# Paired output products in a segment-recurrent transformer kernel, and a new order of its first tiles

## The chip, the cores and the metric

The kernel runs on one core of a Trainium2 chip. The metric is the device time of one launch in microseconds (us), less being better. Each kernel is run several times, and the median is told; in addition one execution is recorded by the hardware profiler. The engines of the core are TensorE (PE; its weight loads are listed as PEld), VectorE (DVE), ScalarE (ACT), GpSimd (POOL) and SyncE (SP). SP, ACT and POOL also issue DMA transfers. SBUF is the on-chip memory of 128 partitions; PSUM holds the results of products[...].

## The reference: what is computed

The input `x` has 2048 rows of 1024 columns in bf16. It is normalized once (`xn`), and two branches work on `xn`: a recurrent attention, and an MLP with 3584 hidden columns. The output is the sum of `x` and both branches.

```python
# attention: 64 segments of 32 rows, 8 memory rows carried from one to the next
for s in range(n_seg):
    h = concat([mem, xs])                                   # 8 + 32 rows
    q, k, v = h @ Wq, h @ Wk, h @ Wv                        # 32 heads of 128
    p = softmax(where(mask, q @ k.T * scale, -1e9))
    o = (p @ v) @ Wo                                        # sum over 32 heads
    mem = o[:8];  outs.append(o[8:])
# MLP
h = gelu(xn @ w1 + b1);  b = h @ w2 + b2
return x + attention(xn) + b
```

Segment s + 1 needs the first eight rows of segment s's output. So the 64 segments run one after the other, and each reads all of `Wq`, `Wk`, `Wv` and `Wo` (32 MB).

## The kernel before

**Two stages.** First comes the MLP, in four groups of 512 rows (`for tg in range(4)`, L488). Each group has 28 blocks `fb` of 128 hidden columns (L507 to L529: eight products into one PSUM bank, then ScalarE and VectorE compute the gelu) and then the product with `w2`. Its result, with `x` and `b2` added, goes to memory and comes back later as `res`, the residual of a segment. Then come the 64 segments (L691).

**Start.** The first four tiles of 128 rows are normalized (L462 to L478): statistics by `bn_stats` on VectorE (L351), the square root on ScalarE (L355), the reciprocal on VectorE (L361), and the scaling, for tiles 0 to 2 on ScalarE (`ln_apply_scalar`, L378) and for tile 3 on VectorE (`ln_apply`, L365). TensorE turns each tile by eight transposes (L387), and VectorE and ScalarE copy the halves out of PSUM (L390). The products of the first block (L510) read all four tiles.

**Units and streams.** The weights are cut into 64 units of 128 x 2048 (512 KB each): 16 each of K, Q, V and O. Of these, 46 stay in SBUF. Eighteen don't fit and are read again in each segment through six places (`STREAM_BUFS`); two of them lie in PSUM banks (`kept`) and are copied by VectorE into their place (`copy_bits`, L244), two copies each. `unit_done` (L675) runs when a unit's products are issued: the place is given to the next stream (`start_stream`), whose DMA is issued from SP and waits for TensorE to have read the old one. Of the sixteen O units, numbers 3, 5, 7, 10, 13 and 14 are streamed; 14 is one of the two kept ones.

**A segment.** K, Q and V each make two half passes of eight units. A unit is four products of 512 columns (`product`, L709, issued at L715), each with 32 rows of the result in another quarter of the partitions (`tile_position`), so that the four run side by side. The 32 rows of a pass are the eight memory rows and 24 of the segment's own. Its other eight rows ("left" rows) are handled for four segments at a time: for each half pass, one segment of four makes a second set of products for them. `i4` is the segment's number modulo 4. Scores, the softmax and `values` (L883) are placed between units, through the lists `at`.

**The O stage** (L1006 to L1017). Sixteen units, each for two heads (k = 0 and 1), are summed in one PSUM bank `psX`. In 17 segments (`left_o`: i4 = 1, and the last one) the stationary operand has 64 rows, and a unit is four products of 512 columns in two halves of the partitions. In the other 47 it has 32 rows, and a unit is eight products of 256 columns, four for each head:

```python
(w, i, u), n = unit, 512 if left_o else 256                              # L911
for k in range(2):
    for jq in range(DM // n):
        r, c0 = n // 8 * jq, DM * k + n * jq                             # row, column
```

Between these units stand the `values` of the second half of the heads, whose results (L905: one copy on ScalarE, one on VectorE) are the stationary operand from unit 8 on. With i4 = 3 VectorE also copies the left rows of V at unit 9 (`left_values`, L770).

**From a segment to the next.** After the last unit, ScalarE copies `psX` as bf16 into `o_sb` (L1022). TensorE first makes some products of the next segment ahead that don't need the memory rows (`lead_products`, up to six units for left rows, three of them ahead of `put_mem`), then `put_mem` (L289) turns the eight memory rows, VectorE copies them into `hT` (L293), and the next segment's K products start. VectorE adds `psX` to `res` (L1037), and GpSimd stores the rows (L1070). At the very end twelve stores are issued from SP, ACT and POOL in turn (L1059).

**Order.** The program's order is the written order on each engine (`manual_schedule`), and each engine works through its own list. Three PSUM banks `acc` are shared by all passes: `new_acc` takes the one that was given back first, `let_go` gives one back.

Of the kernel before, what the change touches and what calls it, by code (L numbers as in the profile page):

```python
# [10 lines left out]
BF16 = mybir.dt.bfloat16  # L11
U32 = mybir.dt.uint32
F32 = mybir.dt.float32
ACT = mybir.ActivationFunctionType
ALU = mybir.AluOpType
PSUM = bass.MemoryType.PSUM

P = 128
# [35 lines left out]
STREAM_BUFS = 6  # L54
AT_BANKS, AT_PART = 5, 4
# [32 lines left out]
def kernel(  # L88
# [211 lines left out]
    with tc.tile_pool(name="ma", bufs=2) as ma, tc.tile_pool(name="mps", bufs=6, space=PSUM) as mps:  # L300
# [27 lines left out]
        load_w1(range(2))  # L328
        nc.sync.dma_start(out=b1rows[:, :], in_=B_b1.rearrange("(fc p) -> fc p", p=P))
        load_w1(range(2, 6))  # L330
# [17 lines left out]
        def ln_stats(tt, xt):  # L348
            stats = ma.tile([P, 2, 6], F32, name="ln_stats")
            for c in range(2):  # L350
                nc.vector.bn_stats(out=stats[:, c, :], in_=xt[:, c * 512:c * 512 + 512])  # L351
            nc.vector.bn_aggr(out=mv[:, tt, :], in_=stats[:, :, :])
# [18 lines left out]
        def ln_apply_scalar(tt):  # L371

            xn = ma.tile([P, DM], BF16, name="ln_xn")
            shift = mv[:, tt, 0:1]
            nc.vector.tensor_scalar(
                out=shift, in0=shift, scalar1=rstd[:, tt:tt + 1], scalar2=-1.0, op0=ALU.mult, op1=ALU.mult,
            )
            nc.scalar.activation(  # L378
                out=xn[:, :], in_=xtoks[tt], func=ACT.Identity, bias=shift, scale=rstd[:, tt:tt + 1],
            )  # L380
            return xn

        def turn_x(tt, xn, xnT):
            t = tt % 4
            pT = mps.tile([P, KT, P], BF16, name="pT", bufs=2)
            for kt in range(KT):
                nc.tensor.transpose(pT[:, kt, :], xn[:, kt * P:(kt + 1) * P], ident)  # L387
            for half in range(2):
                cp = nc.scalar.copy if (tt + half) % 2 else nc.vector.tensor_copy
                cp(  # L390
                    out=xnT[half][:, 4 * t:4 * t + 4, :, :].rearrange("p s k t -> p k s t"),
                    in_=pT[:, 4 * half:4 * half + 4, :].rearrange("p k (s t) -> p k s t", t=SEG),
                )
# [68 lines left out]
        def begin(tt):  # L462
            ln_stats(tt, xtoks[tt])
            ln_sqrt(tt, tt + 1)

        def normed(tt):
            ln_rstd(tt, tt + 1)
            return ln_apply_scalar(tt) if tt < 3 else ln_apply(tt)

        begin(0)  # L470
        xns = []
        for tt in range(4):
            if tt < 3:
                begin(tt + 1)
            xns.append(normed(tt))
            if tt > 0:
                turn_x(tt - 1, xns[tt - 1], xnT)
        turn_x(3, xns[3], xnT)  # L478
# [9 lines left out]
        for tg in range(4):  # L488
# [18 lines left out]
            for fb in range(FC):  # L507
                ps = mps.tile([P, 512], F32, name="ps")
                for kt in range(KT):
                    nc.tensor.matmul(  # L510
                        ps[:, :].rearrange("p (s t) -> p s t", t=SEG),
                        lhsT=w1_sb[fb // 2][:, kt, (fb % 2) * P:(fb % 2 + 1) * P],
                        rhs=xnT[kt // 4][:, :, kt % 4, :],
                        start=(kt == 0),
                        stop=(kt == KT - 1),
                    )
# [28 lines left out]
            if not last:  # L545
# [7 lines left out]
                for t in range(4):  # L553
                    ln_stats(4 * tg + 4 + t, xtoks[4 * tg + 4 + t])
# [66 lines left out]
    with tc.tile_pool(name="late", bufs=1) as late, \  # L621
# [16 lines left out]
        def let_go(ps):  # L638
            free_banks.append(bank_of.pop(id(ps))[0])
# [51 lines left out]
        for s in range(NSEG):  # L691
# [216 lines left out]
            def o_product(unit, t, acc):  # L908


                (w, i, u), n = unit, 512 if left_o else 256  # L911
                lhs = outs[i // 4] if left_o else outs[i // 4][:, :, m0:m0 + SEG]
                for k in range(2):
                    for jq in range(DM // n):
                        r, c0 = n // 8 * jq, DM * k + n * jq
# [192 lines left out]
```

## Time and profile before

| What | us |
|---|---|
| Median of 3 runs | 1869.29 (1865.07 to 1869.99) |
| Profiled execution, its own time | 1868.06 |
| Its span, first to last instruction | 1866.3 |
| First product of the first MLP block | at 15.99 |
| First product of segment 0 | at 419.35 |
| PE busy | 1720.2 (92%) |
| PEld busy | 938.3 (50%) |
| DVE busy | 905.1 (48%) |
| ACT busy | 649.4 (35%) |
| POOL busy | 286.7 (15%) |

In the profile a row of a timeline has the start, the duration, the engine, the line, the operation, its operands as "out<-in" with their shapes, the count of instructions merged in the row, and in brackets how long the engine was idle before it and what ended that. A row of the waits tells who waited for whom: the total in us, how often, and the longest. "issue" is idle time that ended without any event that the profile shows. "DMA" in the page's slices is the busy share of the 16 DMA engines, in tenths, in 40 equal slices of the span.

### The profile page before, as it was taken

The numbers are of one execution on the slowest core, as the hardware profiler recorded it, in microseconds if no ns is written. First come the engines' busy times: TensorE is split into PE (matmuls) and PEld (weight loads), VectorE is DVE, ScalarE is ACT, GpSimd is POOL, SyncE is SP. The second block draws the span as 40 slices with busy tenths as digits, with TensorE's granted clock in tenths as the row PEclk, the third lists the DMA queues.
The fourth block names the chain that finished last, engine by engine and source line by source line (L and its number), as shares of the span: only waits on it lengthen the run. The fifth ranks groups of instructions, "written<-read, shape, count | busy, mean of one in ns | idle before, by whom it ended". The sixth has DMA issues, their size and how long they took to land.

```text
span 1866.3 us, 72877 instructions
## 1 busy us (share of the span) xinstructions
PE 1720.2 (92%) x32208; PEld 938.3 (50%) x32228; DVE 905.1 (48%) x2192; ACT 649.4 (35%) x1382; POOL 286.7 (15%) x563
## 2 busy tenths in 40 slices
PE   7999999999999999998899999999898898999987
PEld 3444444445555555555554555555555454545544
DVE  6657483705444444444444444444444444445443
ACT  6434251602333333333333333333333333333333
POOL 0000001401341121111111111111111111111112
PEclk9999999999999999999999999999999999999999
DMA  9921212769999999999999999999999999999998
GB/s 290 311 83 47 54 46 60 255 217 388 401 394 380 395 390 384 387 380 371 369 383 368 390 388 390 365 384 374 379 389 360 369 368 377 387 389 394 388 381 315
DMA packets 229353, 613.13 MB, mean 329 GB/s; under 512 B 46859, under 2 KB 76091, under 8 KB 229036
## 3 DMA queue, kind: packets, MB, share of 16 engines
q1 hardware_dynamic: 207260, 588.06, 83.8%
q0 software_dynamic: 17536, 17.71, 2.9%
q8 instruction: 252, 4.13, 0.9%
q10 hardware_dynamic: 4240, 2.71, 0.5%
q14 instruction: 65, 0.53, 0.1%
HBM read 594.40 MB, written 29.23 MB: 334 GB/s over the span
## 4 chain that ended last, share of the span: by engine, by line
PE 40%; DMA 20%; issue 4%; DVE 4%; ACT 2%; POOL 0%; DVEq 0%; ACTq 0%; SPq 0%; POOLq 0%
PE acc L715 27%; PE acc L919 9%; DMA u<-Wc_K 8%; DMA u<-Wc_O 7%; DMA outL_d<-half_home 2%; PE acc L891 1%; DMA u<-Wc_Q 1%; ACT mixed L865 1%; DVE b_oL L780 1%; PE mixed L824 1%; DVE pd_main L872 1%; DMA u<-Wc_V 1%; DMA hr_home<-hr_d 1%; ACT mixed L862 0%; PE mixed L830 0%
## 5 line engine op out<-in xcount | busy, mean ns | idle before, releaser
L715 PE MATMUL acc<-u,hr_home 128*32 128x512 bf16 x11520 | 781.3, 381 | 36.6 <-issue 13.8
L715 PEld LDWEIGHTS <-hr_home 128*32 128x32 bf16 x12288 | 353.3, 96 | 321.8 <-issue 69.7
L715 PE MATMUL acc<-u,hrL 128*32 128x512 bf16 x2880 | 258.7, 383 | 7.7 <-issue 7.3
L510 PE MATMUL ps<-u 128*128 128x512 bf16 x896 | 195.5, 381 | 2.6 <-ACT u L390 2.6
L244 DVE TENSOR_SCALAR u<-kept 128x512 uint32<-128x512 uint32 x254 | 163.4, 685 | 33.1 <-PE acc L715 11.1
L919 PE MATMUL acc<-u,d_oL 128*32 128x256 bf16 (+1 forms) x3108 | 157.6, 290 | 22.5 <-DMA u<-Wc_O 12.8
L565 PE MATMUL ps<-u 128*128 128x512 bf16 x657 | 146.2, 379 | 0.8
L919 PEld LDWEIGHTS <-b_oL 128*32 128x32 bf16 x3569 | 112.8, 98 | 67.4 <-issue 36.7
L1070 POOL DMA_DIRECT2D out_dram<-hr_home x188 | 96.3, 513 | 310.3 <-DVE hr_home L1037 296.9
L510 PEld LDWEIGHTS <-u 128*128 128x128 bf16 x896 | 88.1, 98 | 108.8 <-issue 4.8
L919 PEld LDWEIGHTS <-d_oL 128*32 128x32 bf16 (+1 forms) x3552 | 104.4, 98 | 74.9 <-issue 34.9
L872 DVE TENSOR_TENSOR pd_main<-half_home,mixed 128x320 bf16<-128x320 bf16 x128 | 62.5, 488 | 153.5 <-ACT mixed L865 152.2
L919 PE MATMUL acc<-u,b_oL 128*32 128x256 bf16 (+2 forms) x2062 | 119.9, 289 | 18.4 <-DMA u<-Wc_O 10.6
L266 POOL DMA_DIRECT2D hr_home<-hr_d x58 | 32.8, 565 | 589.3 <-PE acc L715 570.0
L780 DVE STREAM_TRANSPOSE b_oL<-b_oL 128x512 bf16<-128x512 bf16 x128 | 90.6, 708 | 63.0 <-ACT b_oL L766 63.0
L715 PEld LDWEIGHTS <-hrL 128*32 128x32 bf16 x3072 | 91.8, 96 | 58.3 <-issue 22.3
L766 ACT CAST kT<-acc 128x512 bf16<-128x512 f32 x64 | 37.5, 586 | 217.2 <-PE acc L715 217.2
L766 ACT CAST b_oL<-acc 128x512 bf16<-128x512 f32 x128 | 75.2, 587 | 83.6 <-PE acc L715 82.6
L565 PEld LDWEIGHTS <-u 128*128 128x128 bf16 x672 | 65.3, 98 | 77.4 <-DVE g_u L526 0.4
L1022 ACT CAST d_oL<-acc 128x256 bf16<-128x256 f32 (+1 forms) x63 | 26.9, 427 | 211.8 <-PE acc L919 211.8
L518 ACT ACTIVATE g_xb<-ps,b1col 128x512 bf16<-128x512 f32 x112 | 76.8, 686 | 60.4 <-PE ps L510 59.3
L865 ACT ACTIVATE mixed<-mixed,small_consts 128x160 f32<-128x160 f32 x256 | 94.2, 368 | 8.4
(127 smaller groups left out, 2004.7 us busy)
## 6 DMA issues: line engine op xcount, KB each, us to landing
u<-Wc_K SPq DMA_DIRECT2D x320, 512.0 KB
u<-Wc_V SPq DMA_DIRECT2D x256, 512.0 KB
u<-Wc_O SPq DMA_DIRECT2D x256, 512.0 KB
u<-Wc_Q SPq DMA_DIRECT2D x128, 512.0 KB
u<-Wc_O SPq DMA_DIRECT2D x64, 320.0 KB
u<-in_B_w_dram SPq DMA_DIRECT2D x28, 512.0 KB
hr_home<-hr_d POOLq DMA_DIRECT2D x58, 128.0 KB, 5.5
u<-in_A_Wq_dram SPq DMA_DIRECT2D x14, 512.0 KB
```

The costliest lines, as they stand in the source:

```text
L244: nc.vector.tensor_single_scalar(out=out, in_=in_, scalar=0, op=ALU.bitwise_or)
L266: eng.dma_start(out=hr_home[:, 0:n], in_=hr_d[s, :, 0:n])
L510: nc.tensor.matmul(ps[:, :].rearrange("p (s t) -> p s t", t=SEG), lhsT=w1_sb[fb // 2][:, kt, (fb % 2) * P:(fb % 2 + 1) * P], rhs=xnT[kt // ...
L518: nc.scalar.activation(out=xb[:, :], in_=ps[:, :], func=ACT.Identity, bias=b1col[:, fb:fb + 1], scale=1.0)
L565: nc.tensor.matmul(ps[:, :], lhsT=gts[fc // 4][:, fc % 4, t * P:(t + 1) * P], rhs=w2_sb[fc // 2][:, fc % 2, cs], start=(fc == 0), stop=(fc ...
L715: nc.tensor.matmul(o, lhsT=lhs[:, i, :], rhs=m, start=(i == seq[0]), stop=(i == seq[-1]), tile_position=(0, 32 * j),)
L766: cp(out=out, in_=ps.rearrange("p (h e) -> p h e", e=32))
L780: nc.vector.transpose(out=home, in_=home)
L865: nc.scalar.activation(out=mixed[:, 160 * b:160 * b + 160], in_=mixed[:, 0:160], func=ACT.Exp, scale=-1.0, bias=off[:, b:b + 1],)
L872: nc.vector.tensor_tensor(out=pdA.rearrange("p c b q -> p b c q"), in0=prA[:, None, :, :].to_broadcast([P, 2, 4, 40]), in1=dd, op=ALU.mult,)
L919: nc.tensor.matmul(acc[r:r + n // 8, c:c + wide], lhsT=lhs[:, 4 * (i % 4) + 2 * u + k, :], rhs=w_t[:, c0 + c:c0 + c + wide], start=(unit = ...
L1070: nc.gpsimd.dma_start(out=out_flat[rows, 256 * j:256 * j + 256], in_=res[32 * j:32 * j + NX, :])
```

## The change

- In the 47 segments that are not `left_o`, O units 0 to 8 (`NPAIR = 9`) are four products of 512 columns. Head k = 0 is summed in partitions 0 to 63 of the bank and head k = 1 in 64 to 127; each product takes 32 partitions and two 256-column blocks of the weights (`r` and `r + 2`) through a strided operand. Units 9 to 15 are eight products of 256 columns as before, into a second bank.
- Ahead of unit 9 `fold` adds the two halves of the first bank: two ScalarE copies and two VectorE additions of 64 x 256 into an f32 tile `folded` in SBUF. At the end VectorE adds the second bank and `folded` into `o_sb`, where ScalarE copied before, and `res` is added to `o_sb` and no longer to PSUM.
- All four first tiles are scaled on VectorE; the statistics are computed by half tiles, and the next tile's half stands between. Sixteen products of the identity (`WARM`) are issued first and never read. The first three MLP blocks are made in halves: the 256 columns of tiles 0 and 1 for two blocks ahead of tile 3's transposes, for the third after them, and then the other halves.
- The bias rows' load stands after the first `w1` tile and not after two. The last stores are issued from SP and ACT alone.

```diff
-        load_w1(range(2))
+        load_w1(range(1))
         nc.sync.dma_start(out=b1rows[:, :], in_=B_b1.rearrange("(fc p) -> fc p", p=P))
-        load_w1(range(2, 6))
+        load_w1(range(1, 6))
...
+        idle = new_ps()
+        for _ in range(WARM):
+            nc.tensor.matmul(
+                idle.rearrange("p (a b) -> p a b", b=P), lhsT=ident, rhs=ident[:, None, :].to_broadcast([P, 4, P]),
+                start=True, stop=True,
+            )
+        begun = [new_ps() for _ in range(3)]
+        ln_stats(0)
+        ln_half(1, 0)
+        ln_sqrt(0, 1)
+        pTs = []
         for tt in range(4):
+            ln_rstd(tt, tt + 1)
+            pTs.append(turned(ln_apply(tt)))
             if tt < 3:
-                begin(tt + 1)
-            xns.append(normed(tt))
-            if tt > 0:
-                turn_x(tt - 1, xns[tt - 1], xnT)
-        turn_x(3, xns[3], xnT)
+                ln_half(tt + 1, 1)
+                turned_out(tt, pTs[tt], 0, xnT, nc.scalar.copy)
+                ln_sqrt(tt + 1, tt + 2)
+                turned_out(tt, pTs[tt], 1, xnT, nc.scalar.copy)
+            if tt < 2:
+                ln_half(tt + 2, 0)
+            if tt == 2:
+                for fb in range(2):
+                    first_product(begun[fb], fb, xnT, 0, 8)
+        turned_out(3, pTs[3], 0, xnT, nc.vector.tensor_copy)
+        turned_out(3, pTs[3], 1, xnT, nc.scalar.copy)
+        first_product(begun[2], 2, xnT, 0, 8)
...
+                if tg == 0 and fb < len(begun):
+                    ps = begun[fb]
+                    first_product(ps, fb, xnT, 8, 16)
+                else:
+                    ps = new_ps()
+                    first_product(ps, fb, xnT, 0, 16)
...
+                for k in range(2):
+                    if left_o:
+                        tiles = [(64 * r, 64, (2 * r, 2 * r + 1)) for r in range(2)]
+                        start, stop = n == 0 and k == 0, n == 15 and k == 1
+                    elif n < NPAIR:
+                        tiles = [(64 * k + 32 * r, 32, (r, r + 2)) for r in range(2)]
+                        start, stop = n == 0, n == NPAIR - 1
+                    else:
+                        tiles = [(32 * r, 32, (r,)) for r in range(4)]
+                        start, stop = n == NPAIR and k == 0, n == 15 and k == 1
+                    for r0, rows, blocks in tiles:
+                        for c, wide, cols in o_columns(unit, t, k, blocks):
                             nc.tensor.matmul(
-                                acc[r:r + n // 8, c:c + wide],
+                                acc[r0:r0 + rows, c:c + wide],
                                 lhsT=lhs[:, 4 * (i % 4) + 2 * u + k, :],
-                                rhs=w_t[:, c0 + c:c0 + c + wide],
...
+            def fold(ps):
+                t = sp.tile([P, 256], F32, name="folded", tag="a")
+                for b in range(2):
+                    nc.scalar.copy(out=t[64 * b:64 * b + 64, :], in_=ps[64:128, 256 * b:256 * b + 256])
+                for b in range(2):
+                    q = slice(64 * b, 64 * b + 64)
+                    nc.vector.tensor_tensor(out=t[q, :], in0=ps[0:64, 256 * b:256 * b + 256], in1=t[q, :], op=ALU.add)
+                let_go(ps)
+                return t
...
+                if n == NPAIR and not left_o:
+                    st["folded"] = fold(psX)
+                    psX = new_acc()
+                o_product(n, t, psX)
...
-                nc.scalar.copy(out=o_sb[:, 0:no, :], in_=psX[:, 0:32 * no].rearrange("p (h e) -> p h e", e=32))
+                o = psX[:, 0:32 * no].rearrange("p (h e) -> p h e", e=32)
+                if left_o:
+                    nc.scalar.copy(out=o_sb[:, 0:no, :], in_=o)
+                else:
+                    folded = st["folded"].rearrange("p (h e) -> p h e", e=32)
+                    nc.vector.tensor_tensor(out=o_sb[:, 0:no, :], in0=o, in1=folded, op=ALU.add)
...
-                engines = [nc.sync, nc.scalar, nc.gpsimd]
+                engines = [nc.sync, nc.scalar]
```

## The prediction

> **What bounds the kernel now.** I read the page's slices first, then the stretches, the waits, and the timeline of one segment and of the first 20 us. The profiled execution took 1868.06 us: a span of 1866.3 and 1.76 around it. It lies 1.2 below the median of the runs shown.
>
> From the page: DMA by slice, and the instruction queue (packets, MB, share).
>
> ```profile
> DMA  9921212769999999999999999999999999999998
> ...
> q8 instruction: 252, 4.13, 0.9%
> ```
>
> From 420 us on, through all 64 segments, the DMA engines are full. Two groups of four segments (busy us and count of each engine, TensorE clock, DMA share, GB/s):
>
> ```profile
> 652.00:740.00 88.00, 81.08 (x1905) 47.32 (x1897) 41.42 (x99) 30.29 (x71) 13.59 (x26) 1.00 1.01 388
> ...
> 1363.00:1452.00 89.00, 79.99 (x1877) 45.84 (x1877) 40.74 (x97) 28.75 (x66) 13.02 (x25) 0.98 0.98 375
> ```
>
> TensorE is 91% busy, DMA at 100%: two resources, both near their limit. The DMA reaches about 400 GB/s when it never runs dry (page: up to 401) and averages 380 to 385. So it starves for some 4% of the time, when TensorE is late in freeing one of the six stream places. What makes TensorE late, from the waits (us in total, times, longest):
>
> ```profile
> PE acc L919 <- DMA u<-Wc_O: 23.3, 57, 1.0
> PE acc L715 <- issue: 23.2, 35, 2.2
> ...
> PE acc L919 <- issue: 18.1, 26, 2.7
> ...
> PE acc L897 <- issue: 3.6, 5, 1.4
> ```
>
> "issue" is idle time that no semaphore ends. All rows together it is 55 us in 81 idles, all in the segments. They have one cause. The page counts 32208 matmuls and 32228 weight loads; divided by the 252 packets that is 256 a packet (4.13 MB/252 = 16.4 KB). Counting TensorE's instructions in the trace, every one of the 81 idles falls at the same place modulo 256 (193 or 194), and ends 1.2 to 1.6 us after the end of an instruction packet. TensorE has run through its block before the next one came through the full DMA engines.
>
> What such an idle costs: cutting the trace at the copies of L1022, the fourteen groups of four segments from 540.5 to 1794.0 us take 86.5 to 92.1 us, with 0.2 to 6.8 us of issue idle. The slope is 0.70 us of group per us of idle (by single segments 0.57); the idle for DMA falls as the issue idle rises (correlation -0.65). I use 0.65: the DMA takes back the rest.
>
> **The paired products.** In 47 of 64 segments (all but `left_o`) units 0 to 8 are 4 products of 512 columns instead of 8 of 256. Two timelines, products by 256 and a product pass by 512:
>
> ```profile
> 666.68 0.84 PE L919 MATMUL acc<-u,d_oL 128*32 128x256 bf16 x24 [0.59 <-issue]
> ...
> 632.33 1.91 PE L715 MATMUL acc<-u,hr_home 128*32 128x512 bf16 x32
> ```
>
> Twenty-four by 256 are three units: (0.84 - 0.40)/2 = 0.22 us each, with 0.40 for one alone. Thirty-two by 512 are eight units: (1.91 - 0.40)/7 = 0.216. So the array time of a unit does not change. [...] By the rows above it is 0, and I take 0[...].
>
> What is left is the code. 47 x 9 x 8 = 3384 instructions fewer (order of the two programs on TensorE: 64458 to 61154, with 80 new ones at the start). That is 13 blocks fewer of 252. More counts where they go: the O stage is the densest stretch, 16 instructions in 0.22 us, so that 256 last 3.5 us, against 7 us in K, Q and V. Now units 0 to 8 have 8 in 0.22. To size it, I took the trace without its issue idles, slid a block of 256 over it, and set its running time against the measured delays from the point where a block is asked for to its landing (median 4.7 us at 600 to 900 us, 3.4 us after 1500). With 0.9 us added, chosen so that before comes to its 53 us after 600 us, the same sum without the 3384 instructions gives 31: 23 us of idle less. The shortest hundredth of the blocks lengthens from 4.0 to 4.7 us. Bounds: 0, if delay grows with use; 55, if all idle goes.
>
> [...] by the 81 idles, 23 x 0.65 = 15 us. The trace decides: the fetch is not hidden where DMA is full.
>
> **The fold and the tail.** At unit 9 ScalarE copies 2 x (64x256) from PSUM, VectorE adds 2 x (64x256), and at the end VectorE adds PSUM and `folded` into `o_sb` where ScalarE copied. No row has 64 partitions; nearest are L1022's 0.37 us for 256 columns on ScalarE and L1037's 0.42 on VectorE (bounds half to once: 0.2 and 0.42 each). I take the full values, two adds in 0.76. ScalarE is idle there ([2.89] below): 0. TensorE goes on into another of the three banks, once L905 has emptied it. With i4 = 0 and 2 this is ScalarE's copy, for which unit 8 waits already; with i4 = 3 VectorE's, done 0.13 us after unit 9 would begin (692.34 below), hidden by the longer wait that follows. VectorE is the question, since its queue is in order. Segment 11 (i4 = 3):
>
> ```profile
> 691.85 0.49 DVE L905 CAST b_oL<-acc 128x320 bf16<-128x320 f32 x1 [2.37 <-PE acc L897]
> 692.26 1.28 DVE L244 TENSOR_SCALAR u<-kept 128x512 uint32<-128x512 uint32 x2
> 693.46 0.68 DVE L770 CAST VL<-acc 128x512 bf16<-128x512 f32 x1
> 694.26 0.37 ACT L1022 CAST d_oL<-acc 128x256 bf16<-128x256 f32 x1 [2.89 <-PE acc L919]
> 694.68 0.12 PEld L289 LDWEIGHTS <-d_oL 128*32 128x32 bf16 x7 [0.25 <-ACT d_oL L1022]
> ```
>
> The two adds queue behind L244, and L770 and the last add behind them: 693.5 + 0.76 + 0.68 = 694.98, and 0.42 for the add is 695.40, where the copy was done at 694.63. `put_mem`, and all of the next segment's K products behind it on TensorE, come 0.77 us later, beyond the lead products. The same sum in every segment: i4 = 3 (15 of them) 8.0 us together, 0.2 to 0.7 each (least where O waited for DMA); i4 = 0, 0.3 in all, since VectorE is just free in time; i4 = 2, 0. The 0.05 us by which the add is longer than the copy hides behind three lead products (0.65 us). So 8.3 x 0.65 = +5.4 us; with the adds at half price the delays sum to 3.0, which makes +1.9. VectorE's add into `res` reads SBUF now and gets shorter (0.42 before), after the path: 0.
>
> Segments: -15 + 5.4 = -9.6 us.
>
> **The first tiles.** Timeline, with cold matmuls from 15.99 on:
>
> ```profile
> 6.82 1.24 ACT L378 ACTIVATE ln_xn<-u,ln_mv,ln_rstd 128x1024 bf16<-128x1024 bf16 x1
> ...
> 14.28 0.77 PEld L387 LDWEIGHTS <-ln_xn 128*128 128x128 bf16 x8 [0.81 <-DVE ln_xn L365]
> ...
> 15.99 46.35 PE L510 MATMUL ps<-u 128*128 128x512 bf16 x207 [0.54 <-ACT u L390]
> ...
> 18.50 0.15 PEld L510 LDWEIGHTS <-u 128*128 128x128 bf16 x1 [0.28 <-issue]
> 18.93 43.13 PEld L510 LDWEIGHTS <-u 128*128 128x128 bf16 x200 [0.28 <-issue]
> ```
>
> The first eight products of 512 are 0.43 us apart, later ones 0.216 (the granted clock reads 1.00 all the while, so it does not show this). Three blocks `fb` are done at 15.99 + 3.43 + 2 x 1.73 = 22.9 us. After: the 16 idle products start at about 1.5 us (identity at 1.38)[...]. Tile 0: statistics to 5.1, reciprocal and apply (0.11 + 0.55) to 6.35; eight transposes at double pace 0.55, to 7.3. Each next tile: ScalarE copy 0.56, square root 0.29, reciprocal 0.11, apply 0.55, transposes 0.55, four handovers 0.25, = 2.3: 9.6, 11.9. Then two half blocks of 8 x 0.108 = 0.86 each to 13.7; tile 3's transposes to 14.3; one half block, to 15.2; bias transposes and tile 3's ScalarE copy to 15.2; three half blocks, 17.9. That is 5.0 earlier. The first weights are not late: 4.1 MB had moved by 16 us (257 GB/s), 1 MB for x and six 0.5 MB tiles; `b1rows` (2.67 us on SP) now stands ahead of the second tile, which is wanted at 14.3.
>
> Whether the array stays at double pace between the tiles is not in the trace. [...] eight transposes of 1.04 us in each 1.7 to 2.9 us never sped it up. If it falls back, the halves cost about 2.6 more: 2.4. I take 4.3. TensorE is busy for 292.7 of 295 us from 120 to 415, and the late loads follow TensorE's progress, so the gain stays.
>
> **The end.** Twelve last stores on SP and ScalarE, six each, where POOL issued its last at 1862.57; about 0.5 us an issue makes that 1863 to 1864: 0, bounds -1 and +1.
>
> **Sum.** -9.6 - 4.3 + 0 = -13.9: 1868.06 - 13.9 = 1854.2, say **1854 us**, 0.8% under the median.
>
> **Rivals.** *Streams take it back.* For: DMA share 1.00, and the idle for DMA rises when the issue idle falls. Against: the slope of 0.57 to 0.70. Then only the start is won: 1864. *Fetch idle goes for good*: 55 x 0.65 = 36 in place of 15, 1833; for it, 4.7 us against a late delay of 3.4. Against: blocks of scores and values are dense too, and L715's idles stay. *Slower, by VectorE's queue*: if the last add is late in all 47 segments, because L244's copies wait for their slot longer than in this trace, each us is 0.65. It decides from (15 + 4.3)/(47 x 0.65) = 0.63 us on average, against 0.18 in my sum; at 1.2 us it is 1886. Against: with i4 = 2, L244 ended 0.8 us or more ahead of the copy in all 16 segments. *It doesn't do what it says* (as many idles as before, at other blocks): 1868 + 5.4 - 4.3 = 1869.
>
> **Numbers.** Measurement tells 0.3% (1863.7 to 1874.9) from no change. Chances: forecast 0.54, fetch gone 0.12, streams 0.20 (half of it under 1863.7), no fewer idles 0.06, slower 0.08. Faster 0.77, same 0.15, slower 0.08. The forecast's own range is 1845 to 1863 (idle saved 12 to 35 us, start 2.4 to 5). Range for 8 in 10: 1836 to 1870.
>
> **What the profile after would show.** L919's issue idle from 18 to about 8 us and all issue idle to about 32, with 239 instruction packets; more idle for DMA than 40 us; idle at L289 on VectorE in i4 = 3 segments of about 0.7; a first half block at about 12 us, cold or not by 0.21 or 0.11 us a product. It is wrong if the idles do not fall, or if groups of four stay at 89 us though they do.

## The result

| | us |
|---|---|
| Kernel before, median of 6 runs | 1869.33 (1865.07 to 1882.14) |
| Changed kernel, median of 6 runs | 1843.78 (1836.66 to 1853.29) |
| Ratio | 0.9845, 95% interval 0.9812 to 0.9878 |
| Profiled executions, before and after | 1868.06 and 1839.26 |
| Spans, before and after | 1866.3 and 1837.5 |

The changed kernel is 1.55% faster: 25.5 us by the medians, 28.8 by the profiled executions, where 15 and 13.9 were forecast. The time lies inside the range of 1836 to 1870, but just outside the forecast's own 1845 to 1863: the gain is 1.7 times (medians) to 2.1 times (profiled executions) the forecast one. So the question for the experiments was not only whether the mechanism is right, but where the other half comes from.

From the page of the changed kernel, DMA by slice and the instruction queue:

```profile
DMA  9931212769999999999999999999999999999998
...
q8 instruction: 239, 3.92, 0.8%
```

The DMA is as full as before in the segments. The instruction packets are 239, the predicted number. The stretches of the changed kernel (busy us and count of each engine, TensorE clock, DMA share, GB/s), the same two groups of segments as shown of before and then the whole segment stage:

```profile
652.00:740.00 88.00, 81.36 (x1801) 44.40 (x1797) 44.65 (x108) 31.48 (x74) 13.89 (x27) 1.00 1.01 386
1363.00:1452.00 89.00, 82.38 (x1822) 44.14 (x1808) 45.73 (x112) 31.81 (x74) 13.59 (x26) 1.00 1.01 389
...
416.00:1831.00 1415.00, 1309.93 (x28591) 703.51 (x28589) 718.52 (x1731) 503.26 (x1168) 243.98 (x463) 1.00 1.01 388
```

The second row is the one that changed: TensorE is busy 82.4 of 89 us, where it was 80.0, and the DMA moves 389 GB/s, where it moved 375. In each of the two stretches TensorE's issue idle was 3.4 us before and is 1.8 and 1.6 now. What TensorE waits for in the changed kernel (us in total, times, longest):

```profile
PE acc L962 <- DMA u<-Wc_O: 28.9, 62, 1.3
PE acc L739 <- DMA u<-Wc_K: 18.2, 34, 1.9
...
PE acc L739 <- issue: 6.8, 10, 1.3
...
PE mixed L291 <- DVE d_oL L1084: 5.0, 17, 0.7
...
PE acc L739 <- DVE folded L978: 3.0, 13, 0.2
...
PE acc L962 <- issue: 1.1, 2, 0.7
```

L962 is the product of O (L919 before), L739 that of K, Q and V (L715). Their issue idle was 18.1 and 23.2 us and is 1.1 and 6.8. Two waits are new: `put_mem` (L291) for the last addition (L1084), and the next segment's first products for the fold's additions (L978), 8.0 us together. Summed over all rows of the segment stage (idles of TensorE over 150 ns):

| | before | after | difference |
|---|---|---|---|
| First product of segment 0 at | 419.35 | 417.42 | -1.9 |
| Segment stage, to the end of the span | 1446.9 | 1420.0 | -26.9 |
| Idle, "issue" (times) | 55.0 (81) | 17.1 (32) | -37.9 |
| Idle for DMA | 39.4 | 51.2 | +11.8 |
| Idle for VectorE | 19.2 | 28.7 | +9.5 |
| Other idle over 150 ns | 4.7 | 2.8 | -1.9 |
| Busy, and gaps under 150 ns, to the last product | 1322.2 | 1313.9 | -8.3 |
| From the last product to the end | 6.4 | 6.4 | 0 |

So the chip did what the sum says, with one term far larger: the idle at the block boundaries (a block is the 256 TensorE instructions that go with one packet: 61132 products and loads in 239 packets, and 64436 in 252 before) fell by 38 us, not by 23.

### The profile page after: what moved, and what is told of

It is laid out like the page before. It is cut to its first block, busy times and chain, and to the rows that moved or that the text cites. A ratio compares the mean times of both kernels' runs of the same rounds, so it can differ in the third digit from the quotient of the medians.

```text
span 1837.5 us, 69927 instructions
## 1 busy us (share of the span) xinstructions
PE 1717.9 (93%) x30556; PEld 893.2 (49%) x30576; DVE 955.3 (52%) x2330; ACT 663.8 (36%) x1429; POOL 284.4 (15%) x559
## 4 chain that ended last, share of the span: by engine, by line
PE 32%; DMA 18%; DVE 4%; ACT 2%; issue 1%; POOL 0%; DVEq 0%; ACTq 0%; SPq 0%
PE acc L739 22%; DMA u<-Wc_K 10%; PE acc L962 6%; DMA outL_d<-half_home 3%; DMA u<-Wc_O 3%; ACT mixed L889 1%; DVE b_oL L804 1%; PE acc L915 1%; DMA hr_home<-hr_d 1%; DVE pd_main L896 1%; PE mixed L848 1%; DMA u<-Wc_V 1%; ACT mixed L886 1%; DMA u<-Wc_Q 0%; PE mixed L854 0%
## 5 line engine op out<-in xcount | busy, mean ns | idle before, releaser
L739 PE MATMUL acc<-u,hr_home 128*32 128x512 bf16 x11520 | 770.8, 380 | 34.0 <-DMA u<-Wc_K 18.2
L739 PEld LDWEIGHTS <-hr_home 128*32 128x32 bf16 x12288 | 342.1, 96 | 317.3 <-issue 57.3
L739 PE MATMUL acc<-u,hrL 128*32 128x512 bf16 x2880 | 248.8, 379 | 3.0 <-DVE folded L978 3.0
L468 PE MATMUL ps<-u 128*128 128x512 bf16 (+1 forms) x920 | 195.7, 375 | 2.0 <-ACT u L388 2.0
L962 PE MATMUL acc<-u,d_oL 128*32 128x512 bf16 (+1 forms) x1792 | 153.3, 381 | 11.7 <-DMA u<-Wc_O 9.4
L589 PE MATMUL ps<-u 128*128 128x512 bf16 x657 | 146.2, 379 | 0.8
L962 PEld LDWEIGHTS <-b_oL 128*32 128x32 bf16 (+1 forms) x3381 | 108.4, 98 | 74.5 <-issue 35.9
L962 PE MATMUL acc<-u,b_oL 128*32 128x256 bf16 (+2 forms) x2062 | 117.1, 289 | 20.2 <-DMA u<-Wc_O 19.5
L962 PEld LDWEIGHTS <-d_oL 128*32 128x32 bf16 (+1 forms) x2048 | 70.3, 99 | 84.7 <-issue 28.0
L739 PEld LDWEIGHTS <-hrL 128*32 128x32 bf16 x3072 | 82.9, 96 | 51.2 <-issue 7.7
L794 ACT CAST v<-acc 128x512 bf16<-128x512 f32 x128 | 75.1, 587 | 48.9 <-PE acc L739 48.6
```

The lines of the kernel that those rows point to most:

```text
L468: nc.tensor.matmul(ps[:, SEG * s0:SEG * s1].rearrange("p (s t) -> p s t", t=SEG), lhsT=w1_sb[fb // 2][:, kt, (fb % 2) * P:(fb % 2 + 1) * P ...
L589: nc.tensor.matmul(ps[:, :], lhsT=gts[fc // 4][:, fc % 4, t * P:(t + 1) * P], rhs=w2_sb[fc // 2][:, fc % 2, cs], start=(fc == 0), stop=(fc ...
L739: nc.tensor.matmul(o, lhsT=lhs[:, i, :], rhs=m, start=(i == seq[0]), stop=(i == seq[-1]), tile_position=(0, 32 * j),)
L794: cp(out=t[:, :], in_=ps[:, :])
L962: nc.tensor.matmul(acc[r0:r0 + rows, c:c + wide], lhsT=lhs[:, 4 * (i % 4) + 2 * u + k, :], rhs=cols, start=start, stop=stop, tile_position ...
```

## The experiments

The kernels were run in three groups, each on one chip with the kernel before beside it. The two halves, the full split and the tail stood beside a median of 1870.63 us; less DMA, the half split and the single run with idle products at the start beside 1870.23; the kernels of the last section beside 1871.58. All ratios are to the kernel before of the same group.

### The two halves of the change, each alone

The start alone is the changed kernel without pairs and fold, and with the three queues for the last stores:

```diff
-NPAIR = 9
+NPAIR = 0
...
-                if n == NPAIR and not left_o:
-                    st["folded"] = fold(psX)
-                    psX = new_acc()
...
-                if left_o:
-                    nc.scalar.copy(out=o_sb[:, 0:no, :], in_=o)
-                else:
-                    folded = st["folded"].rearrange("p (h e) -> p h e", e=32)
-                    nc.vector.tensor_tensor(out=o_sb[:, 0:no, :], in0=o, in1=folded, op=ALU.add)
+                nc.scalar.copy(out=o_sb[:, 0:no, :], in_=o)
...
-                engines = [nc.sync, nc.scalar]
+                engines = [nc.sync, nc.scalar, nc.gpsimd]
```

> The new start alone: the first tiles, the idle products and the halves of the first blocks as in the changed kernel, with the O stage and the last stores as before. Code fetch (my theory: the gain is in idle time of TensorE for its own code, which the paired products shorten): only the start's gain, -3.6 us as in the trace of the changed kernel (block 27 at 62.42 in place of 66.05), so about 1865; issue idle as before, about 55 us. Start (rival: the earlier start shifts the streams so that they collide less): most of the 25 us, about 1847, with issue idle well under 40.

Measured: 1870.69 us, ratio 0.9997 (0.9976 to 1.0018). In its profile `fb` 27 of the first group reaches ScalarE at 61.62 us (66.05 before) and segment 0 starts at 416.47 (419.35 before), so 2.9 us are won ahead of the segments. No gain shows in the time; the interval, which reaches to 0.24% below before, leaves room for 4.5 us at most. Its issue idle is 59.2 us in 84 idles, as many as before: the earlier start does not take it away.

The pairs alone have the start of the kernel before and the segments of the changed one:

```diff
-WARM = 16
...
-        for tt in range(4):
-            ln_rstd(tt, tt + 1)
-            pTs.append(turned(ln_apply(tt)))
...
+        for tt in range(4):
+            if tt < 3:
+                begin(tt + 1)
+            xns.append(normed(tt))
+            if tt > 0:
+                turn_x(tt - 1, xns[tt - 1], xnT)
+        turn_x(3, xns[3], xnT)
```

> The O stage alone: pairs, fold, the sum on VectorE and the last stores as in the changed kernel, with the start of before. Code fetch: issue idle about 17 us in place of 55, 38 x 0.65 = -25, the tail with i4 = 3 +4, so about 1848. Start: about 1866.

Measured: 1847.09 us, ratio 0.9869 (0.9832 to 0.9905), with 15.0 us of issue idle. The whole measurable gain is in the segments.

### Is it the number of instructions?

The pair's places, the fold and the tail stay, but each product of 512 columns is issued as two of 256. This brings the 3384 instructions back and nothing else:

```diff
-                            nc.tensor.matmul(
-                                acc[r0:r0 + rows, c:c + wide],
+                            pieces, split = [(c, wide, cols)], not left_o and wide == 512
+                            if split:
+                                pieces = [(256 * h, 256, cols[:, h, :]) for h in range(2)]
+                            for c, wide, cols in pieces:
+                                nc.tensor.matmul(
+                                    acc[r0:r0 + rows, c:c + wide],
```

> The changed kernel with each product of 512 columns in units 0 to 8 issued as two of 256 columns, to the same places in the same bank: the same array time, the same fold, sums and banks, the same start, and 3384 TensorE instructions more (64538 in all). Code fetch: the issue idle comes back to about 50 us, and the time to that of before with the start's gain and the tail's cost, 1869 - 3.6 + 4 = about 1870. Rival (the gain is in what else changed in the segments: the first bank free at unit 9, the residual read from SBUF, one engine fewer at the end): it keeps its gain, about 1844.

Measured: 1865.92 us, ratio 0.9978 (0.9957 to 0.9998). Its instruction queue and its waits:

```profile
q8 instruction: 252, 4.13, 0.9%
```

```profile
PE acc L739 <- issue: 24.9, 36, 2.2
...
PE acc L966 <- issue: 16.5, 24, 1.8
```

All rows together the issue idle is 53.3 us in 78 idles. The arithmetic, its places and the tail are those of the changed kernel. Only the 3384 instructions are back, and 22 us of its gain have gone (1865.92 against 1843.78; both stand beside a kernel before of 1869 to 1871). Units 0 to 4 alone split in this way (1880 instructions more) give the dose between:

```diff
-                            pieces, split = [(c, wide, cols)], not left_o and wide == 512
+                            pieces, split = [(c, wide, cols)], not left_o and wide == 512 and n < 5
```

> The changed kernel with O units 0 to 4 split into twice as many products at the same places (1880 instructions more), units 5 to 8 left whole; fold and tail as in the changed kernel. Theory (idle goes with the number of blocks and with how short they are, by and by): issue idle between 32 and 42 us (17 plus 1880/3384 of the 36 us between the changed kernel and the one with all nine split), time about 1856 us. Rival (a threshold: only the shortest blocks, those that lie wholly in O, stall): issue idle within 6 us of the changed kernel's 17 or of the split one's 53, and the time 1845 or 1865.

Measured: 1857.39 us, ratio 0.9935 (0.9904 to 0.9966), with 32.4 us of issue idle in 50 idles and 247 packets. Time and idle lie between the two ends, where the theory put them (the idle at the lower edge of its 32 to 42 us): the threshold of the rival is not there.

### What is the tail worth?

With i4 = 3 the copy of the left rows' V at unit 9, which stands in VectorE's queue ahead of the last addition, goes to ScalarE:

```diff
-                    at[9] = [lambda: left_values(1, psV1L)]
+                    at[9] = [lambda: left_values(1, psV1L, nc.scalar.copy)]
```

> The changed kernel with the copy of V's left rows at unit 9 (i4 = 3) on ScalarE in place of VectorE. If VectorE's queue sets the end of those segments, as the order of its work says, put_mem comes 0.5 us after the last product there and not 1.26; TensorE's idle for it and for the fold (6.8 us in 15 segments) goes, and 6.8 x 0.65 = -4 us: about 1840. If the streams take it back: 1844, with more idle for DMA.

Measured: 1843.56 us, ratio 0.9858 (0.9805 to 0.9911). The wait that was aimed at is nearly gone; from the waits of this kernel:

```profile
PE mixed L291 <- DVE d_oL L1084: 1.0, 2, 0.5
...
PE acc L739 <- DVE folded L978: 3.0, 13, 0.2
```

This row lost 4.0 us, and with i4 = 3 `put_mem` starts 0.76 us after the last O product instead of 1.26 (mean of 15; 0.5 was expected). The time is that of the changed kernel within what can be measured. By 0.65 us of time per us the 4.0 should give 2.6 us, which is 0.14%: too little to see here. Nor did TensorE's idle for VectorE as a whole fall in this profile (28.7 to 30.6 us): K products wait twice, for 3.4 and 2.2 us, for VectorE's copy at L295 behind a late load of rows; in the changed kernel's profile such waits are 0.6 us at most. The expectation of 1840 is neither met nor refuted.

### Is it the full DMA?

The theory says that TensorE waits at a block boundary because the instruction packet comes through full DMA engines. Then with less DMA the change should be worth nothing. The same edit was made in both kernels. After the first pass, the five streamed K units take a tile that lies in SBUF, and 512 KB each are not read again; the K products then use other weights.

```diff
         n = starts.popleft()
+        if streams[n][0] == "K" and n >= STREAMED:
+            stream_tiles[n], slot_of[n] = res_tiles[UNIT_AT["low0"]], slot
+            return
         unit, t = streams[n], slab(slot)
```

> The kernel before, but after the first pass of the resident K units the five streamed K units of each segment take a tile that lies in SBUF (they multiply other weights than they should) and their 512 KB are not read again: 2.6 of 8.5 MB per segment less DMA, with the same instructions on TensorE. Theory (TensorE waits at block boundaries because the instruction packet comes through full DMA engines): the issue idle of 55 us and the DMA idle of 39 us both nearly go, and the time is about 1775 us (1866 less some 90), with at most 5 us of issue idle. Rival (a block boundary costs by itself, however busy the DMA is): the issue idle stays at 50 us or more, only the DMA idle goes, and the time is about 1825.

> The changed kernel with the same edit as in the run before this one. Theory (the fewer instructions help only because the DMA is full): with nothing left to save, this one is within 6 us of the kernel before with less DMA: about 1775 us, the start's 2 to 4 us against 5 to 10 us of the tail of segments with i4=3, which the DMA no longer hides. Rival (an instruction costs by itself, in overhead on the array or at block boundaries): it keeps most of its lead and is 20 us or more below the kernel before with less DMA.

Measured: 1785.47 us (ratio 0.9550, 0.9523 to 0.9578) for the kernel before with less DMA and 1783.67 (0.9538, 0.9516 to 0.9561) for the changed one. The segment stage in the stretches of the first and of the second:

```profile
416.00:1775.00 1359.00, 1288.19 (x30291) 735.64 (x30289) 665.59 (x1593) 486.70 (x1122) 244.78 (x465) 1.00 0.79 283
```

```profile
416.00:1775.00 1359.00, 1289.23 (x28590) 688.53 (x28589) 713.50 (x1732) 503.17 (x1167) 243.89 (x463) 1.00 0.80 283
```

With the DMA at 80% instead of 100%, the lead of 25 us shrinks to 1.8, as the theory said and the rival did not: 3384 instructions fewer are by themselves worth nothing that is seen. But the theory's number for the idle was wrong. Without the change the issue idle fell from 55.0 to 26.7 us, not to 5, and in the changed kernel it is 15.0. The two are equal in time because the changed kernel pays those 11.7 us back: 7.2 us more idle for VectorE (the tail) and 6.9 more for DMA. So a full DMA makes about half of the boundary idle, and fewer instructions save some of it at 80% too, only without a gain in time. What makes the rest when the DMA is at 80% was not tried.

### Does the array stay at double pace in the start?

In the changed kernel's timeline the array slows between tiles 1 and 2:

```profile
8.69 0.62 PE L383 MATMUL pT<-hr_home,ln_xn 128*128 128x128 bf16 x8 [1.65 <-DVE ln_xn L374]
11.04 1.04 PE L383 MATMUL pT<-hr_home,ln_xn 128*128 128x128 bf16 x8 [1.73 <-DVE ln_xn L374]
11.87 3.19 PE L468 MATMUL ps<-u 128*128 128x256 bf16 x16
```

Eight transposes took 0.62 us for tile 1 and 1.04 for tile 2, and sixteen half products 3.19. This kernel has idle products between the tiles as well:

```diff
             pTs.append(turned(ln_apply(tt)))
+            if tt < 2:
+                keep_busy(6)
```

Here `keep_busy(n)` is the loop of the `WARM` products with n in place of 16.

> The changed kernel with six more products of the identity behind the transposes of tiles 0 and 1, so that TensorE has work while it waits for the next tile. Theory (the array falls back to half pace because it is idle for most of each 2.3 us between tiles): the eight transposes of tile 2 take 0.6 us instead of 1.04, the sixteen half products 0.11 us each instead of 0.2, and the block with fb=27 reaches ScalarE about 1.3 us earlier, at 61.1 instead of 62.4 us. Rival (the fall has another cause, such as a clock that is lowered from outside at that time): the half products stay at 0.2 us each. The time of the launch moves by less than can be measured.

Its timeline:

```profile
9.16 0.62 PE L383 MATMUL pT<-hr_home,ln_xn 128*128 128x128 bf16 x8 [0.35 <-DVE ln_xn L374]
...
11.51 0.62 PE L383 MATMUL pT<-hr_home,ln_xn 128*128 128x128 bf16 x8 [0.43 <-DVE ln_xn L374]
11.96 1.91 PE L468 MATMUL ps<-u 128*128 128x256 bf16 x16
```

The half products are 0.11 us apart now ((1.91 - 0.2)/16), and `fb` 27 reaches ScalarE at 61.39 us instead of 62.42, as the theory said. But these are two launches, and other profiles show that the added products did not make the difference. This is the second profile of the changed kernel, without them (from the run "changed, again" below):

```profile
10.04 0.62 PE L383 MATMUL pT<-hr_home,ln_xn 128*128 128x128 bf16 x8 [1.65 <-DVE ln_xn L374]
12.39 0.62 PE L383 MATMUL pT<-hr_home,ln_xn 128*128 128x128 bf16 x8 [1.73 <-DVE ln_xn L374]
12.85 1.91 PE L468 MATMUL ps<-u 128*128 128x256 bf16 x16
```

The idle times are the same as in the first profile, and the array stays at double pace. The stretch from 11.06 us on, in the first and in the second profile (the granted clock is the third number from the end):

```profile
11.06:14.47 3.41, 3.41 (x21) 2.67 (x22) 1.44 (x4) 1.25 (x3) 0.29 (x1) 0.50 1.20 290
```

```profile
11.06:14.47 3.41, 2.08 (x23) 1.93 (x24) 2.35 (x7) 2.15 (x6) 0.59 (x2) 1.00 1.19 293
```

Seven profiles have this start without added products. Two fell to half clock at 11.06 us (the changed kernel's first and the one with less DMA); five did not fall. In the two, the trace's record of the granted clock reads full from 4.2 us on; in the five it does so from a moment between 6.0 and 7.5 us. The three profiles with added products did not fall either. So idle times of this size are not enough for a fall, and whether the added products can prevent one stays open. They win nothing else: in all eight profiles without a fall, with added products or without, `fb` 27 stands at 58.62 or 58.63 us plus half of the time at which the clock became full (in this kernel's run 5.52 us, which makes 61.39). A fall costs another 1.6 to 1.7 us.

The single time of this kernel was 1860.70 us, above every run of the changed kernel.

### Does it matter where the boundaries fall?

Six products in two places are 24 instructions, which move all block boundaries of the segments by 24 places. Four segments of the changed kernel hold 3578 products and loads, and the trace has another two to three semaphore instructions a segment, so the boundaries (every 256; 14 x 256 = 3584) nearly stand still from group to group. In the kernel before (3794) they slide. So the places of the changed kernel could be lucky ones, and those of the kernel with the added products bad ones. That kernel was timed, without an edit:

> The kernel of the one look with twelve more idle products, unchanged, now timed, since its single time of 1860.7 us lay above all runs of the changed kernel. Its 24 more instructions move every block boundary of 256 in the segments by 24 places, and the changed kernel's four segments hold 3578 instructions, 6 short of 14 blocks, so that its boundaries nearly stand still from group to group. Theory A (where the boundaries fall doesn't matter; the one look was the spread of single runs): median 1840 to 1847, issue idle 15 to 22 us. Theory B (it matters, and the changed kernel's places are lucky ones): median 1855 or more, issue idle near the 28.7 us of the one look.

The next one moves the boundaries by 128:

```diff
             pTs.append(turned(ln_apply(tt)))
+            if tt < 2:
+                for _ in range(32):
+                    nc.tensor.matmul(idle[:, 0:32], lhsT=ident, rhs=ident[:, 0:32], start=True, stop=True)
```

> The changed kernel with 32 products of 32 columns (64 instructions) behind the transposes of each of tiles 0 and 1: all block boundaries of the segments move by 128, half a block. Theory A (places don't matter): median within 0.4% of the changed kernel, 1837 to 1850, issue idle 14 to 24 us. Theory B (they do): the issue idle is outside that, up to 35 us if these places are bad ones, and each us of it is 0.65 us, so up to 1856.

> The changed kernel once more, unedited, beside the two moved ones on the same chip. Both theories: 1840 to 1847 us. Its issue idle beside the 17.1 us of its first profile says how far one profile of one kernel differs from another: theory A needs 5 us or more between them to explain a part of the one look's 28.7; theory B needs under 5.

| Kernel (boundaries moved by) | median, us | runs | ratio (95%) | issue idle, us |
|---|---|---|---|---|
| changed, again (0) | 1838.67 | 1832.96 to 1840.28 | 0.9817 (0.9773 to 0.9860) | 18.2 (17.1 in its first profile) |
| moved by 24 | 1848.38 | 1843.52 to 1855.96 | 0.9882 (0.9838 to 0.9927) | 26.1 (28.7 in its single run before) |
| moved by 128 | 1840.75 | 1835.99 to 1842.00 | 0.9833 (0.9797 to 0.9869) | 14.5 |

The kernel moved by 24 has no run as fast as the slowest of the unmoved one on the same chip, and in both of its profiles 8 to 12 us more issue idle than in both of the other's. Its waits show the idles at the K products and in the scores (L853, L859), not in O:

```profile
PE acc L744 <- issue: 9.3, 18, 1.1
...
PE mixed L859 <- issue: 4.2, 5, 1.5
...
PE mixed L853 <- issue: 3.8, 5, 1.2
```

So the place seems to matter for this shift: 9.7 us beside the unmoved kernel. How much of that comes from the place is less sure. At 0.65 us each, 8 us of idle are 5 us. Both moved kernels have a wait of some 4 us at 567 us, for VectorE's copy at L295 behind a late load of rows, which neither profile of the unmoved one has. The kernel of the tail experiment, which has the same TensorE instructions as the unmoved one, has 21.5 us of issue idle. And in the first comparison the unmoved kernel had a median of 1843.78, only 4.6 us under that of the moved one. The medians lay between what A and B had expected, the idle on B's side. But the changed kernel isn't a lucky exception: moved by 128, and with the start of before (15.0 us of idle; 80 instructions fewer ahead of the segments), it has as little idle. The single run's 1860.70 is not explained by the place alone; its granted clock was also lower over the whole span (0.992 against 0.996), with six stretches of 3.41 us at half clock in the segments where the timed kernel's profile has two. Why a shift of 24 is bad was not found.

## Why the prediction was right, and where it was wrong

**What bounds it, and the mechanism: right.** All issue idle was to fall from 55 to about 32 us and that of O's products from 18 to about 8; it fell to 17.1 and 1.1. All 32 issue idles of the changed kernel again begin at place 193 to 195 modulo 256 of TensorE's instructions, counted with the semaphore instructions, and end 1.3 to 1.6 us after an instruction packet (5th to 95th percentile). The split kernel shows that the instruction count makes the gain. The pair with less DMA shows that the gain in time needs the full DMA; the idle falls without it too (26.7 to 15.0 us).

**Array time of a pair: about 0, as taken.** With less DMA, where little idle hides it, TensorE's busy time differs by 1 us between 30291 and 28590 products (1288.2 and 1289.2 us in the two stretches above), and the times by 0.1%. The 7.2 us (1316.9 to 1309.7) by which TensorE's busy time fell at full DMA were not foreseen. About half is the clock: its record has three stretches of 3.41 us at half clock in the segments before (from 442, 1166 and 1405 us on) and one after (1155), and two such stretches make 3.4 us. The rest is not explained.

**The size of the saved idle: this is the step that failed.** "The same sum without the 3384 instructions gives 31: 23 us of idle less." Measured: 17.1, and 37.9 less. Two things were wrong with that sum. First, I had counted places by products and weight loads alone; the semaphore instructions count as well, and by the end of the trace the place at which I took the delays was some 75 places off. Counted rightly, the median delay is not 4.7 us early and 3.4 late but 5.2 (600 to 900 us) and 5.5 (after 1500). Done again with the right count, and scaled to the same 55 us, the sum gives 27 left and 28 saved. That is 5 of the missing 15. Second, it set every block against the same delays. To see what that left out, each block of the segments is sorted by the time TensorE takes, without its issue idle, from the place at which I take it to be asked for (153, ahead of which no packet starts in the traces before and after) to its beginning (place 193 of the block after: 296 instructions). The delay runs from that place to the end of the packet:

| Time to run | before: blocks, idle, median delay | after | all nine split |
|---|---|---|---|
| under 5.5 us | 26, 19.5 us, 4.4 to 5.0 | 0 | 19, 13.2 us, 4.1 to 4.7 |
| 5.5 to 6 | 25, 10.0 us, 5.03 | 25, 4.6 us, 4.68 | 27, 12.5 us, 4.76 |
| 6 to 7 | 91, 21.1 us, 5.34 | 92, 11.2 us, 4.73 | 97, 21.2 us, 5.24 |
| over 7 | 88, 4.5 us, 5.51 | 103, 1.3 us, 5.65 | 86, 5.2 us, 5.65 |

The shortest blocks are gone, as I had said, and with them 19.5 us. The other 18 come from blocks that are as many and as long as before: those of 5.5 to 7 us lost half of their idle, and their packets come 0.35 and 0.6 us sooner. The rows are not sharp: counting from a place or two further or less moves blocks to the next row, and the first row before then holds 16 to 22 us. In the second profile of the changed kernel this is weaker in the third row (5.07 us of delay, 11.9 us of idle), so a shorter median is not all of it. The bound that I gave for this term (55 us, if all idle goes) held it; I chose too near the other end, and 37.9 lies outside the 12 to 35 us of my own range too. Why the delays got shorter is not settled.

**Time per us of idle: near.** The split kernel gives the best price, since its start and tail are those of the changed one: 36.2 us more idle (17.1 to 53.3) and 22.1 us more time, 0.61 by the medians and 0.69 by the ratios. By groups of four segments the slope in the changed kernel is 0.64 in its first profile and 0.76 in its second (0.70 before), but it hangs on the segment at which the groups begin: 0.23 to 0.64 and 0.18 to 0.79. 37.9 x 0.65 = 24.6 is what the term should have been. The idle for DMA rose by 11.8 us to 51.2, where "more than 40 us" was forecast.

**The tail: mechanism and size right.** Segment 11 of the changed kernel (i4 = 3), VectorE's queue at the end of O:

```profile
688.95 1.28 DVE L246 TENSOR_SCALAR u<-kept 128x512 uint32<-128x512 uint32 x2
...
690.15 0.84 DVE L978 TENSOR_TENSOR folded<-acc,folded 64x256 f32<-64x256 f32 x2
...
691.02 0.69 DVE L794 CAST VL<-acc 128x512 bf16<-128x512 f32 x1
...
691.74 0.42 DVE L1084 TENSOR_TENSOR d_oL<-acc,folded 128x256 bf16<-128x256 f32 x1
692.22 0.12 PEld L291 LDWEIGHTS <-d_oL 128*32 128x32 bf16 x8 [0.75 <-DVE d_oL L1084]
```

The order is the predicted one: copies, fold, left V, last addition. The additions of the fold take 0.42 us each, the full price taken and not half of it, and the addition into `res` takes 0.29 us where it took 0.42 (medians of L1104 in these 47 segments, and of L1037). `put_mem` starts 1.26 us after the last O product with i4 = 3 (mean of 15), where it started after 0.47: 0.79 later, against 0.77 in the sum. TensorE's idle at L291 is 5.0 us in 17 waits, less each than the 0.7 us that I had named; with that behind the fold it is 8.0 us, against 8.3. That it costs 0.65 of this was not shown: half of it was taken away at no visible change. The rival in which VectorE's queue decides is refuted: with i4 = 0 and 2, `put_mem` comes after 0.55 and 0.52 us.

**The start: 3.6 us instead of 4.3, and 1.9 left.** `fb` 27 comes 3.63 us earlier. The first half block stands at 11.87 us (about 12 forecast), and its products are cold, 0.2 us apart. The 4.3 was a price between two cases (5.0 at double pace, 2.4 cold). Both cases occur, so it is a middle and no knowledge of which: in the seven profiles with this start the gain at `fb` 27 is 3.6 to 4.4 us. The fall itself lasted 3.41 us and cost 1.7, where 2.6 was priced. In two of the seven profiles the array fell to half pace though no idle between the tiles was longer than 1.73 us, and in five it did not; what decides this was not shown. In the changed kernel's first profile TensorE worked for 0.62 of the 4.0 us between tile 0's transposes and tile 2's (7.04 to 11.04 us), and the fall came at 11.06. "The granted clock reads 1.00 all the while" was a misreading: the record of before begins at 19.08 us, about when the products become fast, and what lies ahead of it counts as 1.00. "The gain stays" was wrong in the profiled run. From 360 to 400 us, with TensorE busy 39.59 us in both, the granted clock was 0.96 in the changed kernel (one stretch of 3.41 us at half clock, which is 1.7 us) and 1.00 before, and segment 0 starts only 1.93 us earlier. The kernel before has such a stretch at 442 us, already in the segments. Segment 0 starts at 416.5 to 417.4 us in the seven profiles with this start, and at 419.1, 419.4 and 422.5 in the three with the old one.

**The end: 0, as taken.** From the last product to the end of the span it is 6.4 us in both.

**The sum, with measured terms:** 37.9 x 0.65 = -24.6, tail 8.0 x 0.65 = +5.2, start -1.9, together -21.3. The profiled executions differ by 28.8 and the medians by 25.5. The 7.2 us of busy time named above are the largest part of what is still missing. The measured term of 24.6 us lies about midway between the forecast's 15 and the 36 of the rival "fetch idle goes for good" (1833 us in all); "streams take it back" and "as many idles as before" are refuted by the time and by the row of issue idle in the table at the top. (The 1886 us of "slower" should have been 1885 by its own numbers.)

## What to carry to other kernels

When an engine idles with no releaser, count its instructions: idles that all stood at one place modulo 256 (193 to 195) were waits for code here, and under a full DMA instructions saved in the densest stretch were time (1843.78 us, and 1865.92 with the 3384 back), though they saved the array nothing. Size such a saving with both effects, fewer short blocks and packets that come sooner; holding the measured delays fixed gave 23 us here where 38 were saved. And before one works on a new wait of some us that the trace shows clearly, one should ask whether a us of idle is a us of time: half of this tail's idle was removed and no run could tell. A change in the first microseconds should not be read from one launch against another: the moment at which the clock becomes full moved the same code by more than a microsecond (tile 1's transposes started at 8.69 and at 10.04 us).

## What was not expected of the hardware

- A shift of all block boundaries by 24 instructions, with the segments' work unchanged, went with 9.7 us (1838.67 to 1848.38, four runs each on one chip), one by 128 with 2.1. So a kernel compared with its neighbour may differ by up to half a per cent for a reason other than what the edit was meant to change.
- With 31% less to read (2.6 of 8.5 MB a segment), TensorE's busy time in the segments of the kernel before fell from 1316.9 to 1286.2 us, with the same 30281 products and the same granted clock (0.996 and 0.997). There are 89 idles fewer (238 to 149); if each costs the 0.18 us by which a lone unit's row is longer than one in a run (0.40 against 0.22), that is 16 of the 31 us. One stretch at half clock fewer is 1.7. The rest is open.
- The 16 identity products took 4.99 to 6.59 us in ten profiles of kernels that begin with the same sixteen, and the granted clock became full between 4.2 and 7.5 us. Each us later puts `fb` 27 half a us later; but the two earliest, at 4.2 us, were followed by a fall to half clock, and came out like the latest.
- TensorE's busy time in the segments goes with the stretches of 3.41 us at half clock that the clock's record has there. The seven profiles of kernels with the paired products at full DMA have 1307.3 us with none, 1309.7 with one, 1310.0 to 1311.1 with two, 1312.6 with three and 1318.8 with six.
